# Another order of the first loads and a new hand-planned list of first steps in a fused attention and expert kernel

## The chip, the cores and the metric

The kernel runs on one core of one Trainium2 chip. The time is device microseconds of one execution; of several executions the median is given. Four compute engines work side by side, each through its own queue in program order: PE (TensorE), DVE (VectorE), ACT (ScalarE) and POOL (GpSimd). SP, ACT and POOL also issue DMA transfers from their queues.

## The reference

Block-wise linear attention with a decay per head, then a two-layer network with an ELU between the layers.

```python
B, H, S, D = 4, 8, 768, 64          # block = 64, nb = 12
for b in range(nb):
    intra = einsum('bhic,bhjc->bhij', qb, kb) * Dmask        # decay ** (i - j), causal
    intra = einsum('bhij,bhjd->bhid', intra, vb)
    inter = einsum('bhid,bhde->bhie', qb * lam_pow, kv_state)
    out[:, :, sl] = intra + inter
    kv_state = lam_block * kv_state + einsum('bhsd,bhse->bhde', kb * rev_pow, vb)
x = out.transpose(0, 2, 1, 3).reshape(3072, 512)
h = x @ w_in                        # 512 x 2048
g = where(h > 0, h, exp(min(h, 0)) - 1)
return g @ w_out                    # 2048 x 512
```

## The kernel before

A *step* s is one block of 64 positions of a pair of batches: 24 steps, s even for batches 0 and 1, odd for 2 and 3. Partitions 0 to 63 hold the first batch of the pair, 64 to 127 the second. Per step the keys, queries and values arrive as `kn`, `qn`, `vn` in fp16, cast by the transfer (POOL queue, two transfers each, one per batch). Step 0's keys and queries are different: they are loaded uncast as `kraw`, `qraw` over the queues of SP and ACT, and DVE casts them. A *group* is two steps, 256 rows of the network's input.

The two weight matrices come in four blocks each, `wi0` to `wi3` and `wo0` to `wo3`, on the POOL queue, in an order written by hand between the loads of the steps. The scheduler is off (`manual_schedule`): instructions are issued as the Python code calls them. The first steps are called from a string, `start`; behind it a regular loop takes over from group 3. A word of the string is one call:

- `Fk`, `Fq`: casts of step 0 on DVE (`cast0`). `K0`: the decay mask times the causal mask on DVE; `K1`: `lamL` and `powi`, nine exponentials on ACT (`consts`).
- `Aso.us.ss.sx` (`visit`): up to four things on PE, an empty place leaves one out: the outputs O of step so (and, with a state, the state's share I), the state update U of step us, the scores S of step ss, the transposes T of the keys and queries of step sx.
- `C` copies the transposes out of PSUM, `P` multiplies scores by the mask, `V` decays the values (`vd`, for U), `N` writes the new state `st`, `D` decays the state (`sd`), `Q` decays the queries (`qs`, for I): all DVE. `X` copies an O to `xt`, the input of the network, on ACT.
- `Hg.c.n.f` (`mm1_h`): the first layer's matmuls for group g, half c, four of its sixteen column tiles from f (16 matmuls of 128 columns, weights `wi` of block f/4). `E` (`mm1_e`): exp and relu on ACT. `G` (`mm1_g`): the ELU on DVE. `Ms.f` (`mm2`): four of the second layer's sixteen matmuls for step s, weights `wo` of block f/4. `Zs` (`mm2_o`): copy and store of its result.

So `A..1.` is "scores of step 1", `A...2` "transposes of step 2". Scores and state updates share a PSUM tile `psZ` (`psS` and `psU`), the transposes of the first four steps share `psM` with the results of M, the H results `psH` have two buffers, e and r four each. Constants are made from an iota `ij` (POOL; `ident`, `ijf`, `caus`, `i1f` on DVE) and from `lam_b`, the decay bases, loaded on the ACT queue. On ACT one table load stands at the start.

Of the kernel before, what the change touches and what calls it, by code (L numbers as in the profile page):

```python
# [8 lines left out]
FP32 = mybir.dt.float32  # L9
# [7 lines left out]
def kernel(  # L17
# [10 lines left out]
    nc = tc.nc  # L28

    B, H, S, D = q.shape  # L30
    L = 64
# [10 lines left out]
    cst = ctx.enter_context(tc.tile_pool(name="cst", bufs=1))  # L42
    inp = ctx.enter_context(tc.tile_pool(name="inp", bufs=1))
# [6 lines left out]
    def where(s):  # L50
        return 2 * (s % NPR), s // NPR

    def half(x):
        return slice(64 * x, 64 * x + 64)

    lam_b = cst.tile([128, H], FP32, name="lam_b")
    nc.scalar.dma_start(out=lam_b[:], in_=lam.unsqueeze(0).broadcast_to([128, H]))
    nc.scalar.preload_act_table_set("natural_log_exp_and_others")

    NB = 12  # L60
    kn, qn, vn = {}, {}, {}

    def load(which, s):
        b, c = where(s)
        src, keep, tag = {"k": (k, kn, "kn"), "q": (q, qn, "qn"), "v": (v, vn, "vn")}[which]
        keep[s] = inp.tile([128, H, D], FP16, tag=tag, bufs=NB, name=f"{tag}{s}")
        for r in range(2):
            nc.gpsimd.dma_start(  # L68
                out=keep[s][half(r)],
                in_=src[b + r, :, c * L : (c + 1) * L, :].rearrange("h p d -> p h d"),  # L70
            )

    def load_step(s):
        load("k", s)
        load("q", s)
        load("v", s)
# [12 lines left out]
    def load_wo(i):  # L89
# [2 lines left out]
            in_=moe_w_out[i * WB : (i + 1) * WB, :].rearrange("(g p) f -> p g f", p=128),  # L92
        )

    ij = cst.tile([128, L], I32, name="ij")
    for r in range(2):
        nc.gpsimd.iota(ij[half(r)], pattern=[[1, L]], base=0, channel_multiplier=-1)

    raw0 = {}
    for which, src in (("k", k), ("q", q)):  # L100
        raw0[which] = inp.tile([128, H, D], FP32, name=f"{which}raw0")
        for r in range(2):
            (nc.sync if which == "k" else nc.scalar).dma_start(
                out=raw0[which][half(r)], in_=src[r, :, 0:L, :].rearrange("h p d -> p h d")
            )
    load("v", 0)
    load_step(1)
    load_wi(0)
    load_step(2)
# [29 lines left out]
        out=i1f[:], in0=raw[:], scalar1=rjf[:, 0:1], scalar2=float(L),  # L139
# [276 lines left out]
    def consts(i):  # L416
# [13 lines left out]


    start = (
        "Fk Fq V0 A...0 C0 A.0.. K1 N0 A...1 K0 A..0. P0 V1 A0... X0 D2 A.1.. N1 H0.0.1.0 C1 D3 "
        "A..1. E0.0.1.0 P1 A...2 A1... C2 X1 Q2 A..2. H0.1.1.0 P2 E0.1.1.0 V2 A2... G0.0.1.0 "
        "A.2.. H0.0.1.4 X2 N2 H1.0.1.0 E0.0.1.4 D4 G0.1.1.0 A...3 E1.0.1.0 H1.0.1.4 C3 Q3 A..3. "
        "E1.0.1.4 H0.1.1.4 V3 G0.0.1.4 E0.1.1.4 P3 H0.1.1.8 G1.0.1.0 H0.0.1.8 E0.1.1.8 G0.1.1.4 "
        "A.3.. G1.0.1.4 A3... E0.0.1.8 H1.0.1.8 N3 M1.0 D5 X3 G0.0.1.8 E1.0.1.8 H1.1.1.0 G0.1.1.8 "
        "M0.0 E1.1.1.0 G1.0.1.8 H0.1.1.12 G1.1.1.0 H1.1.1.4 E0.1.1.12 M1.4 E1.1.1.4 G0.1.1.12 "
        "H1.1.1.8 H0.0.1.12 G1.1.1.4 E1.1.1.8 M1.8 E0.0.1.12 G1.1.1.8 H1.0.1.12 G0.0.1.12 A...4 "
        "E1.0.1.12 H1.1.1.12 C4 M0.4 V4 E1.1.1.12 G1.0.1.12 M0.8 Q4 A..4. G1.1.1.12 M1.12 P4 "  # L440
        "M0.12 Z1 M2.0 Z0 A...5 V5 M2.4 C5 M3.0 Q5 A4.4.5.6 M3.4 P5 X4 N4 H2.0.1.12 C6 H2.0.1.4 "
        "E2.0.1.12 Q6 M3.8 D6 E2.0.1.4 H2.0.1.8 G2.0.1.12 V6 M3.12 E2.0.1.8 G2.0.1.4 A5.5.6.7 V7 "
        "Z3 G2.0.1.8 H2.0.1.0 X5 N5 H2.1.1.12 E2.0.1.0 P6 M2.8 D7 E2.1.1.12 G2.0.1.0 H2.1.1.4 V8 "
        "M2.12 E2.1.1.4 G2.1.1.12 H2.1.1.0 C7 Z2 G2.1.1.4 A6.6.7.8 E2.1.1.0 Q7 M4.0 N6 X6 "
        "G2.1.1.0 M4.4 P7 H2.1.1.8 C8 M4.8 E2.1.1.8 D8 Q8 A7.7.8.9 G2.1.1.8 M4.12 X7 N7 P8 Z4 C9 "
    )
    steps = {
        "C": att_C, "P": att_P, "X": lambda s: att_X(s, nc.scalar),
# [87 lines left out]
```

## Time and profile before

| | |
|---|---|
| median of 3 runs | 219.03 us (218.57 to 219.05) |
| profiled execution | 218.62 us, of it span 216.8 us |
| PE busy | 201.8 us, 93% of the span |
| DVE, ACT, POOL busy | 152.8, 134.0, 135.7 us |
| first matmul | at 8.06 us |
| first matmul of the network (H) | at 13.14 us |
| moved by DMA | 20.73 MB, of it 13.38 over the POOL queue |

The span goes from the first to the last instruction; about 1.8 us lie around it. Times inside the profile are microseconds from the start of the span. A row of the time line gives the start, the length, the engine, the line of the kernel, the operation, what it writes and reads, how many instructions are merged in it and, in brackets, how long the engine had been idle and who ended that. Lengths of instructions overlap: on DVE an operation of 0.68 us is followed by the next start 0.6 us later, on ACT one of 0.59 us by the next 0.49 us later.

### The profile page before, as it was taken

The numbers are of one execution on the slowest core, as the hardware profiler recorded it, in microseconds if no ns is written. First come the engines' busy times: TensorE is split into PE (matmuls) and PEld (weight loads), VectorE is DVE, ScalarE is ACT, GpSimd is POOL, SyncE is SP. The second block draws the span as 40 slices with busy tenths as digits, with TensorE's granted clock in tenths as the row PEclk, the third lists the DMA queues.
The fourth block names the chain that finished last, engine by engine and source line by source line (L and its number), as shares of the span: only waits on it lengthen the run. The fifth ranks groups of instructions, "written<-read, shape, count | busy, mean of one in ns | idle before, by whom it ended". The sixth has DMA issues, their size and how long they took to land.

```text
span 216.8 us, 8162 instructions
## 1 busy us (share of the span) xinstructions
PE 201.8 (93%) x3600; PEld 143.0 (66%) x3600; DVE 152.8 (70%) x224; ACT 134.0 (62%) x259; POOL 135.7 (63%) x180
## 2 busy tenths in 40 slices
PE   0479989999999999999999999999999999999992
PEld 0358868657867677677676676676676676666662
DVE  3788884859987789769779769779769748433321
ACT  4633867526756677577577577577577577567730
POOL 8988525997999799797797797797734102000000
PEclk9999999999999999999999999999999999999999
DMA  7999999999999959977986976977921121122024
GB/s 105 144 178 176 180 205 180 135 146 130 141 140 132 123 73 75 105 85 59 106 88 57 106 86 56 107 85 59 104 53 22 33 51 23 30 48 48 3 48 98
DMA packets 84436, 20.73 MB, mean 96 GB/s; under 512 B 77104, under 2 KB 81456, under 8 KB 84400
## 3 DMA queue, kind: packets, MB, share of 16 engines
q0 software_dynamic: 78144, 13.38, 79.5%
q1 hardware_dynamic: 4896, 6.43, 13.0%
q10 hardware_dynamic: 1360, 0.40, 0.9%
q8 instruction: 28, 0.46, 0.9%
q14 instruction: 8, 0.07, 0.1%
HBM read 27.27 MB, written 6.29 MB: 155 GB/s over the span
## 4 chain that ended last, share of the span: by engine, by line
PE 90%; POOL 4%; DMA 3%; issue 1%; DVE 1%; ACT 1%; POOLq 0%; DVEq 0%
PE psH L347 39%; PE psM L387 38%; PE psO L304 3%; DMA qn<-in_q_dram 3%; PE psO L273 2%; PE psM L406 2%; PE psZ L297 2%; POOL vn L68 1%; PE psZ L290 1%; POOL kn L68 1%; PE psO L282 1%; POOL qn L68 1%; PE psO_None L273 1%; PE psM L304 0%; PE psO_None L282 0%
## 5 line engine op out<-in xcount | busy, mean ns | idle before, releaser
L368 DVE SCALAR_TENSOR_TENSOR g<-e,r 128x512 f16<-128x512 f32 x96 | 84.0, 889 | 45.7 <-ACT r L359 45.4
L347 PE MATMUL psH<-xt,wi 128*128 128x256 f16 (+1 forms) x960 | 101.2, 256 | 0.8 <-DMA wi<-in_moe_w_in_dram 0.6
L347 PEld LDWEIGHTS <-wi 128*128 128x128 f16 x960 | 80.8, 100 | 25.0 <-DMA wi<-in_moe_w_in_dram 0.7
L357 ACT ACTIVATE e<-psH 128x512 f32<-128x512 f32 x96 | 57.4, 598 | 60.1 <-PE psH L347 59.7
L387 PE MATMUL psM<-wo,g 128*128 128x512 f16 x368 | 93.7, 380 | 0.0
L359 ACT ACTIVATE r<-psH 128x512 f16<-128x512 f32 x96 | 57.0, 594 | 0.0
L387 PEld LDWEIGHTS <-g 128*128 128x128 f16 x368 | 33.9, 98 | 25.2
L68 POOL DMA_DIRECT2D vn<-in_v_dram x48 | 34.3, 751 | 5.5 <-DMA wo<-in_moe_w_out_dram 3.0
L201 POOL TENSOR_TENSOR qs<-T,powi 128x512 f16<-128x512 f16 x14 | 16.3, 1164 | 33.1 <-DVE T L222 33.1
L68 POOL DMA_DIRECT2D kn<-in_k_dram x46 | 32.6, 731 | 3.1 <-DMA wo<-in_moe_w_out_dram 2.3
L68 POOL DMA_DIRECT2D qn<-in_q_dram x46 | 32.3, 729 | 1.5 <-DMA kn<-in_k_dram 0.9
L192 POOL TENSOR_TENSOR sd<-st,lamL 128x512 f32<-128x512 f16 x12 | 17.8, 1487 | 0.0
L208 DVE TENSOR_TENSOR P<-psZ,mask 128x512 f16<-128x512 f32 x24 | 16.4, 683 | 1.8 <-PE psZ L297 0.9
L394 ACT COPY o<-psM 128x512 f32<-128x512 f32 x23 | 13.6, 592 | 4.9 <-PE psM L387 4.9
L183 DVE TENSOR_TENSOR vd<-vn,rev 128x512 f16<-128x512 f16 x22 | 15.0, 682 | 0.0
L244 DVE TENSOR_TENSOR st<-psZ,sd 128x512 f16<-128x512 f32 x20 | 13.6, 680 | 0.8 <-PE psZ L290 0.8
L232 ACT CAST xt<-psO 128x512 f16<-128x512 f32 x18 | 10.6, 587 | 4.7 <-PE psO L304 4.5
L304 PEld LDWEIGHTS <-qn 64*64 64x64 f16 x384 | 6.6, 109 | 9.4 <-DVE qn L171 8.1
L222 DVE COPY T<-psO 128x1024 f16<-128x1024 f16 x18 | 12.2, 680 | 0.0
L273 PEld LDWEIGHTS <-st 64*64 64x64 f16 x352 | 6.9, 106 | 5.5 <-issue 2.6
L304 PE MATMUL psM<-ident,qn 64*64 64x64 f16 x64 | 2.1, 231 | 8.4 <-DVE qn L171 8.1
L273 PE MATMUL psO<-qs,st 64*64 64x64 f16 x288 | 9.4, 202 | 0.0
(47 smaller groups left out, 110.7 us busy)
## 6 DMA issues: line engine op xcount, KB each, us to landing
out_dram<-o SPq DMA_DIRECT2D x46, 128.0 KB, 2.5
vn<-in_v_dram POOLq DMA_DIRECT2D x48, 64.0 KB, 3.8
kn<-in_k_dram POOLq DMA_DIRECT2D x46, 64.0 KB, 4.1
qn<-in_q_dram POOLq DMA_DIRECT2D x46, 64.0 KB, 3.4
wi<-in_moe_w_in_dram POOLq DMA_DIRECT2D x4, 512.0 KB, 6.5
wo<-in_moe_w_out_dram POOLq DMA_DIRECT2D x4, 512.0 KB, 11.1
kraw<-in_k_dram SPq DMA_DIRECT2D x2, 128.0 KB, 4.3
qraw<-in_q_dram ACTq DMA_DIRECT2D x2, 128.0 KB, 4.6
```

The costliest lines, as they stand in the source:

```text
L68: nc.gpsimd.dma_start(out=keep[s][half(r)], in_=src[b + r, :, c * L : (c + 1) * L, :].rearrange("h p d -> p h d"),)
L183: eng.tensor_tensor(out=st[s]["vd"][:], in0=vn[s][:], in1=rev[:].unsqueeze(2).broadcast_to([128, H, D]), op=ALU.mult,)
L192: eng.tensor_tensor(out=st[s]["sd"][:], in0=state[s - NPR][:], in1=lamL[:].unsqueeze(3).broadcast_to([128, 2, NHP, D]), op=ALU.mult,)
L201: eng.tensor_tensor(out=st[s]["qs"][:], in0=st[s]["T"][:, :, 1, :, :], in1=powi[:], op=ALU.mult)
L208: nc.vector.tensor_tensor(out=d["P"][:].rearrange("p y j t -> p y (j t)"), in0=psS, in1=mask[:].rearrange("p y j t -> p y (j t)"), op=ALU. ...
L273: return nc.tensor.matmul(O[half(c), y, h // 2 * L : (h // 2 + 1) * L], lhsT=state[so - NPR][half(x), y, 2 * i + c, :], rhs=st[so]["qs"][h ...
L304: return nc.tensor.matmul(psT[r][half(c), x : x + L], lhsT=(kn, qn)[i][sx][half(r), NHP * (c ^ r) + j, :], rhs=ident[half(r), :], is_trans ...
L347: nc.tensor.matmul(psH[:, i, :], lhsT=wi[n // 4][:, kk, (n % 4) * 128 : (n % 4 + 1) * 128], rhs=xt[grp][:, kk, c0 * 128 : c0 * 128 + T], s ...
L357: nc.scalar.activation(e[:], psH[:], AF.Exp)
L359: nc.scalar.activation(r[:], psH[:], AF.Relu)
L368: nc.vector.scalar_tensor_tensor(out=g[:], in0=e[:], scalar=-1.0, in1=r[:], op0=ALU.add, op1=ALU.min)
L387: nc.tensor.matmul(acc[s], lhsT=gel.pop((s, n)), rhs=wo[n // 4][:, n % 4, :], start=(n == 0), stop=(n == NFT - 1),)
```

## The change

The first loads are issued in another order. On the ACT queue the first half of the queries goes first, then `lam_b`, then the second half, then the table load; before, `lam_b` and the table load stood ahead of both halves. On the POOL queue the two transfers of step 0's values go ahead of the two iotas instead of behind them. On the SP queue the two halves of the keys are issued as before. The string `start` is replaced by another order of the same 182 words.

```diff
-    lam_b = cst.tile([128, H], FP32, name="lam_b")
-    nc.scalar.dma_start(out=lam_b[:], in_=lam.unsqueeze(0).broadcast_to([128, H]))
-    nc.scalar.preload_act_table_set("natural_log_exp_and_others")
...
+    raw0 = {}
+    for which in "kq":
+        raw0[which] = inp.tile([128, H, D], FP32, name=f"{which}raw0")
+    lam_b = cst.tile([128, H], FP32, name="lam_b")
+    for r in range(2):
+        for which, src, eng in (("k", k, nc.sync), ("q", q, nc.scalar)):
+            eng.dma_start(
+                out=raw0[which][half(r)], in_=src[r, :, 0:L, :].rearrange("h p d -> p h d")
+            )
+        if r == 0:
+            nc.scalar.dma_start(out=lam_b[:], in_=lam.unsqueeze(0).broadcast_to([128, H]))
+    nc.scalar.preload_act_table_set("natural_log_exp_and_others")
+    load("v", 0)
     ij = cst.tile([128, L], I32, name="ij")
     for r in range(2):
         nc.gpsimd.iota(ij[half(r)], pattern=[[1, L]], base=0, channel_multiplier=-1)
-
-    raw0 = {}
-    for which, src in (("k", k), ("q", q)):
-        raw0[which] = inp.tile([128, H, D], FP32, name=f"{which}raw0")
-        for r in range(2):
-            (nc.sync if which == "k" else nc.scalar).dma_start(
-                out=raw0[which][half(r)], in_=src[r, :, 0:L, :].rearrange("h p d -> p h d")
-            )
-    load("v", 0)
     load_step(1)
     load_wi(0)
...
     start = (
-        "Fk Fq V0 A...0 C0 A.0.. K1 N0 A...1 K0 A..0. P0 V1 A0... X0 D2 A.1.. N1 H0.0.1.0 C1 D3 "
-        "A..1. E0.0.1.0 P1 A...2 A1... C2 X1 Q2 A..2. H0.1.1.0 P2 E0.1.1.0 V2 A2... G0.0.1.0 "
-        "A.2.. H0.0.1.4 X2 N2 H1.0.1.0 E0.0.1.4 D4 G0.1.1.0 A...3 E1.0.1.0 H1.0.1.4 C3 Q3 A..3. "
-        "E1.0.1.4 H0.1.1.4 V3 G0.0.1.4 E0.1.1.4 P3 H0.1.1.8 G1.0.1.0 H0.0.1.8 E0.1.1.8 G0.1.1.4 "
-        "A.3.. G1.0.1.4 A3... E0.0.1.8 H1.0.1.8 N3 M1.0 D5 X3 G0.0.1.8 E1.0.1.8 H1.1.1.0 G0.1.1.8 "
...
+        "Fk Fq K1 K0 A...0 C0 V0 A..0. A...1 P0 V1 A.0.. A0... X0 N0 C1 A.1.. N1 D2 H0.0.1.0 D3 "
+        "A..1. E0.0.1.0 P1 A...2 A1... G0.0.1.0 X1 C2 H0.1.1.0 V2 A..2. Q2 E0.1.1.0 P2 H0.0.1.4 "
+        "G0.1.1.0 A2... E0.0.1.4 A.2.. H0.1.1.4 N2 X2 G0.0.1.4 A...3 E0.1.1.4 H1.0.1.0 C3 V3 "
+        "A..3. E1.0.1.0 H1.0.1.4 P3 Q3 A.3.. E1.0.1.4 H0.0.1.8 G1.0.1.0 D4 A3... E0.0.1.8 "
+        "G1.0.1.4 H0.1.1.8 G0.1.1.4 X3 H1.0.1.8 G0.0.1.8 E0.1.1.8 N3 M1.0 D5 E1.0.1.8 H1.1.1.8 "
...
```

In the part left out, the second-layer steps come in the order M1.0, M2.0, M2.4, M2.8, M1.4, M1.8 (before: M1.0, M0.0, M1.4, M1.8, M0.4, M0.8), the visits keep their order from `A...4` on, and around the visit `A4.4.5.6` DVE is given

```diff
-  ... A4.4.5.6 M3.4 P5 X4 N4 H2.0.1.12 C6 H2.0.1.4 E2.0.1.12 Q6 M3.8 D6 E2.0.1.4 H2.0.1.8 G2.0.1.12 V6 ...
+  ... A4.4.5.6 V6 M0.12 N4 X4 P5 H2.0.1.4 Z0 D6 H2.0.1.12 C6 E2.0.1.4 M3.4 Q6 E2.0.1.12 G2.0.1.4 ... V7 ...
```

## The prediction

> **What bounds the kernel now.** I read the page first, for the shares; then the busy times of PE (TensorE) by stretches; then the chain of waits and the time line of the first 30 us. An execution is bound by PE once PE has work, and the whole change lies before that.
>
> The page, head and slices (each digit a fortieth of the span, 5.4 us):
>
> ```profile
> span 216.8 us, 8162 instructions
> ...
> PE 201.8 (93%) x3600; PEld 143.0 (66%) x3600; DVE 152.8 (70%) x224; ACT 134.0 (62%) x259; POOL 135.7 (63%) x180
> ...
> PE   0479989999999999999999999999999999999992
> ...
> DMA  7999999999999959977986976977921121122024
> ```
>
> The busy time of PE in stretches that I chose (stretch, its length, PE busy and instructions, granted clock, share of the DMA engines, GB/s):
>
> ```profile
> 0.00:8.06 8.06, 0.00 (x0) 1.00 1.27 119
> 8.06:13.14 5.08, 3.16 (x128) 1.00 1.55 155
> 13.14:30.00 16.86, 15.74 (x367) 1.00 1.50 183
> 30.00:70.00 40.00, 40.00 (x817) 1.00 1.60 147
> 70.00:200.00 130.00, 129.93 (x2203) 1.00 0.72 70
> ```
>
> From 30 us PE never rests. Both lists hold the same 182 words in another order, so PE's instructions are the same. An order can change only what PE loses before 30 us: 8.06 + 1.92 us ahead of the first expert matmul (H0.0.1.0, 13.14 us) and 1.12 us between it and 30. It could also add gaps later.
>
> The time line of PE around these losses (start, length, instruction, count, idle before it and its releaser):
>
> ```profile
> 12.13 0.43 PE L290 MATMUL psZ<-vd,kn 64*64 64x64 f16 x16 [0.17 <-DVE vd L183]
> ...
> 13.14 1.89 PE L347 MATMUL psH<-xt,wi 128*128 128x128 f16 x16 [0.58 <-DMA wi<-in_moe_w_in_dram]
> ...
> 16.19 0.43 PE L282 MATMUL psO_None<-P,vn 64*64 64x64 f16 x16
> ...
> 17.33 1.89 PE L347 MATMUL psH<-xt,wi 128*128 128x128 f16 x16
> ...
> 23.16 1.07 PE L347 MATMUL psH<-xt,wi 128*128 128x128 f16 x16
> ...
> 26.65 1.05 PE L347 MATMUL psH<-xt,wi 128*128 128x128 f16 x16 [0.19 <-ACT r L359]
> ...
> 29.04 0.21 PE L282 MATMUL psO_None<-P,vn 64*64 64x64 f16 x1 [0.53 <-issue]
> ```
>
> The first H waits for weight block wi0, with 0.58 us to spare behind the last small matmul: the steps ahead of it are paid by a transfer, not by their order. Secondly, 16 matmuls of one H take 1.89 us at 13.14 and 17.33 but 1.07 from 23.16 (0.18 of either is the tail of the last one): PE starts at half speed. The granted clock reads 1.00 all along, so I go by durations. The two H from 20.23 take 2.56 us to the next start; with 107 ns (1.71/16) and 55.6 ns (0.89/16) per matmul, 15 are slow, so full speed comes at about 21.8 us.
>
> **The change part by part.**
>
> *Queues.* ACT issued lam_b (0.74 us, 0.39 long), then the two halves of q0 from 1.20 (0.73 and 0.65). Now q0's first half goes at 0.74, lam_b behind it at about 1.47, q0's second half at about 1.86 (was 1.95), and the table load (1.28 us) follows at 2.55 instead of 1.17. On POOL the two v0 issues (1.53 us) pass the two iotas (0.40 us): v0 is sent some 0.5 us earlier, the iotas end at about 2.8 instead of 1.24, and k1 goes where it went, 2.89, as the sum ahead of it is the same. SP keeps its order.
>
> *Who waits for the moved small things.* The six DVE constants from the iota (1.27 to 2.24 us) run 1.5 us later and end by 3.8. lam_b took 2.6 us to land; issued at 1.47 that gives 4.1, and if it lands only with q0's first half in front of it, at most some 4.6 (k0's first half, issued at 0.74, needed 4.3 in all), against 3.4 now. The chain loglam, loglamP, eight mask exponentials, which ended at 6.5, then ends at 7.2 to 7.7. The list now puts K0 (mask times causal, 0.68) ahead of the first T copies; it starts at 7.93 behind the two casts and still has its mask in time. If not, the first T copies are late, and of that the spare 0.58 us is free.
>
> *The block up to the first H, laid end to end with the rows of before.* Casts to 8.00; K0 to 8.6; T0 copies at 8.74 (they wait for PE, as now) to 9.41; V0 to 10.0; P0 (S0 on PE ends near 10) to 10.7; V1 to 11.3; N0 to 11.9. PE: O0 ends near 11.2, so X0 ends at 11.85 (now 12.59); U1 needs N0's read of psU and ends at 12.4 (now 12.56). All is ahead of wi0, which landed just under 13.14. Moving V0, K0 and N0 is worth nothing here; cover left 0.7 us.
>
> *When wi0 lands.* The DMA engines hold work without a break from about 2.5 us until far behind wi0. The only gain is that two streams, not one, run from the start. The stretches moved 31 GB/s in 2.0 to 2.5 us, 142 in 2.5 to 3.0 and 216 in 3.0 to 4.0. With q0 beside k0 at once I take 62 and 216: (31 + 74) GB/s over half a microsecond, 52 KB more, which is 0.3 us at the 172 to 185 GB/s behind it. Bounds: 0.46 us (what q0's first issue gains) and, on the side of loss, 0.3 us, should mixed streams or the late lam_b cost what they are to bring. I take 0.3 earlier for wi0 and all that follows on that queue. Until 21.8 PE runs at half speed and does half the work per time, so this is worth 0.15 us at the end.
> [...]
>
> *The new order from 13.14 to 30 us.* Now: H0.0.1.0, S1, T2 (held to 15.52 by q2's landing), O1, S2 in pieces between 16.64 and 17.2 because it waits for T2's two copies, H0.1.1.0 at 17.33. New: H0.1.1.0 stands straight behind O1, and waits for the X1 copy (16.66 to 17.24), so it starts at 17.25, and S2 (0.25 us at half speed) comes after it: a loss of 0.25 - 0.08 = 0.17. What is queued behind this wait on PE is S2 and all later H; DVE loses nothing, P2 is due later. In return H0.0.1.4 now stands between S2 and O2, so P2 and Q2 on DVE stay hidden. Further, H0.0.1.8 at 26.65 waited for ACT to free its buffer (0.19 us idle behind the 0.18 us tail of the matmul before: some 0.35 without a new start), and the two H from 24.41 took 2.05 us for 2 x 0.89 + 0.18 = 1.96; in the new list A.3.. and A3... stand between these H, and ACT's pair per H (0.98 us) keeps up with PE's 0.89 plus 0.2 to 0.6 of attention. Gain 0.35 + 0.09. One H behind A.2.. meets the X2 copy and waits about 0.07. Sum: 0.17 + 0.07 - 0.44 = -0.2 us.
>
> *Later.* The list puts V6 and V7 (decays of v6, v7) earlier on DVE; N4, P5, C6 and the qs of the next visit queue behind V6, two g steps behind V7. v6 was issued by 44.3 and the landing of a v load is 3.8 us in the middle, so V6 waits until about 47; the visit that needs the results starts at 53.3 now. Cover 4 us, cost nothing; without it the visit would be late by the wait.
>
> **Sum.** -0.15 - 0.2 = -0.35 us. The profiled execution took 218.62 us (span 216.8, 1.8 around it), so 218.3 on its scale; the median of the runs is 0.41 higher, 219.03, so I expect 218.7.
>
> **The rivals.**
>
> *The stall at 28.3 goes too.* The last of O3's matmuls started 0.73 us behind its neighbour, with no releaser ("issue"). For its going: nothing in the list explains it, and the new list has another step at that place. Against: if it hangs on the place in PE's instruction stream, it stays. Time: 218.7 - 0.7 = 218.0.
>
> *The longer pause delays full speed: slower.* In the new list PE rests about 0.65 us in one piece ahead of H0.1.1.0, where the old one filled half with S2. If the speed-up at 21.8 hangs on how busy PE was in the stretch before, it may come later; every H at half speed costs 0.82 more. Three of them late give 2.5 us at most, two 1.6, so 220.3 for two. It decides from one and a half H on (1.2 us): below that the gain of 0.35 holds it within measurement. Against: from 17.25 on the new list is denser than the old, and PE's busy share from 17.33 to 21.67 is already 98%.
> [...]
>
> *The loads do nothing, or the order does nothing* (one of the two terms is 0): 218.8 to 218.9, inside my forecast.
>
> **How the numbers follow.** A measurement of this kernel can tell about 0.3%, 0.66 us. My forecast and its weaker forms, 218.4 to 219.3: 0.54. The stall's going, alone or with the upper bound of the loads (0.46 instead of 0.3) and a slightly earlier full speed, 217.4 to 218.3: 0.33. Later full speed or a late mask or wi0, 219.7 to 220.6: 0.13. The range leaves out the far half of each rival: 217.5 to 219.9.
>
> **What would show it.** Right: H0.0.1.0 starts at 12.7 to 13.2 and still waits for wi0; the chain of waits passes through q2 and X1 to H0.1.1.0; the idle time of PE between the first H and 30 us falls from 1.12 by some tenths; no PE idle time from 30 to 70. Wrong: the first H late because of X0 or the mask; H rows of 1.89 us behind 22; PE gaps around 47 to 66 with DVE as releaser.

## The result, and the profile after

The changed kernel is slower: median 220.71 us (219.68 to 221.59, eight executions) against 219.04 (218.52 to 220.1) for the kernel before beside it; ratio 1.0065, 95% interval 1.0036 to 1.0094 (the quotient of the two medians is 1.0076, inside it). I had forecast 218.7 and given "slower" 0.13. Executions that took over 1.5% longer than the fastest of their kernel are left out of all ratios and differences below. The profiled execution of after took 219.68 us, the shortest of the eight: its trace explains 219.68 - 218.62 = 1.06 us of the 1.67 between the medians. For the rest I rely on the runs below.

The page after, the lines shown of before:

```profile
span 217.9 us, 8163 instructions
...
PE 200.6 (92%) x3600; PEld 142.2 (65%) x3600; DVE 153.0 (70%) x224; ACT 134.0 (62%) x259; POOL 135.8 (62%) x180
...
PE   0188989999999999999999999999999999999992
...
DMA  7999999999999949958967967967920120122024
```

The second digit of PE's slices (5.4 to 10.9 us) fell from 4 to 1: the first matmuls come later. The busy time of PE in the same stretches as before:

```profile
0.00:8.06 8.06, 0.00 (x0) 1.00 1.23 118
8.06:13.14 5.08, 2.39 (x112) 1.00 1.32 142
13.14:30.00 16.86, 14.39 (x368) 1.00 1.52 178
30.00:70.00 40.00, 39.82 (x821) 1.00 1.60 144
70.00:200.00 130.00, 129.93 (x2203) 1.00 0.72 71
```

Idle time of PE rose by 0.77 us up to 13.14, by 1.35 between there and 30, and by 0.18 from 30 to 70: 2.30 in all. Its busy time fell by 1.2 (201.8 to 200.6), since less of the work ran at half speed (252 matmuls started ahead of full speed, before 302; one of an H took 107 ns there, 56 behind it): 2.30 - 1.2 = 1.1, the growth of the span. In the third stretch one can see both at once: one instruction more (368 against 367) in 1.35 us less of busy time. The last column matters too: 142 GB/s moved between 8.06 and 13.14, where it had been 155.

The time line (start, length, what, count, idle before it and its releaser), POOL and ACT's queue first, then DVE, then PE:

```profile
1.25 1.54 POOL L64 DMA_DIRECT2D vn<-in_v_dram  x2 [0.81 <-POOLq L523]
1.52 0.68 ACTq L103 DMA_DIRECT2D lam_b<-in_lam_dram  x1
2.88 0.43 POOL L108 IOTA ij<- 64x64 int32 x2
3.25 1.35 POOL L64 DMA_DIRECT2D kn<-in_k_dram  x2
6.39 0.25 DVE L145 TENSOR_SCALAR lam_b<-lam_b 128x8 f32<-128x8 f32 x1 [1.76 <-DMA lam_b<-in_lam_dram]
9.59 0.69 DVE L420 TENSOR_TENSOR mask<-mask,caus 128x512 f32<-128x512 f32 x1 [0.91 <-ACT mask L157]
13.43 0.43 PE L292 MATMUL psZ<-vd,kn 64*64 64x64 f16 x16 [0.58 <-DVE st L250]
13.84 1.89 PE L349 MATMUL psH<-xt,wi 128*128 128x128 f16 x16
...
18.00 1.87 PE L349 MATMUL psH<-xt,wi 128*128 128x128 f16 x16 [0.68 <-ACT xt L234]
...
28.01 1.01 PE L349 MATMUL psH<-xt,wi 128*128 128x128 f16 x15
29.99 1.12 PE L349 MATMUL psH<-xt,wi 128*128 128x128 f16 x17 [0.97 <-issue]
```

The same iotas, issues of POOL and use of `lam_b` in before:

```profile
0.84 0.40 POOL L97 IOTA ij<- 64x64 int32 x2 [0.39 <-POOLq L520]
...
1.38 1.53 POOL L68 DMA_DIRECT2D vn<-in_v_dram  x2
...
2.89 1.38 POOL L68 DMA_DIRECT2D kn<-in_k_dram  x2
3.41 0.17 DVE L143 TENSOR_SCALAR lam_b<-lam_b 128x8 f32<-128x8 f32 x1 [1.16 <-DMA lam_b<-in_lam_dram]
```

Three things stand here that the prediction had otherwise. The iotas, moved behind the values, now lie between two issues of POOL, and step 1's keys go at 3.25 instead of 2.89. `lam_b` was issued at 1.52, close to the 1.47 that I had said, but DVE got it at 6.39 (before 3.4), and the mask chain reaches K0 at 9.59. And the stall without a releaser, 0.73 us at 28.3 before, is longer and stands at 29 (1.19 us from the start of one matmul at 28.80 to that of the next at 29.99).

The chain of waits from the start confirms the second point:

```profile
1.52 4.85 DMA lam_b<-in_lam_dram
...
7.54 2.03 ACT mask L157 x8
...
12.76 0.63 DVE st L250
```

The 4 KB of `lam_b` took 4.85 us to land. Mask, K0, T0's copies (10.20; before 8.74), V0, P0, V1, N0 and U1 follow each other up to the first H at 13.84. Block `wi0` landed at 13.79 (before 13.09) in the same execution: the two causes end within 0.1 us of each other (U1 at 13.86), so undoing one of them alone would have left the start where it was. That is why parts had to be undone one by one.

### The profile page after: what moved, and what is told of

It is laid out like the page before. It is cut to its first block, busy times and chain, and to the rows that moved or that the text cites. A ratio compares the mean times of both kernels' runs of the same rounds, so it can differ in the third digit from the quotient of the medians.

```text
span 217.9 us, 8163 instructions
## 1 busy us (share of the span) xinstructions
PE 200.6 (92%) x3600; PEld 142.2 (65%) x3600; DVE 153.0 (70%) x224; ACT 134.0 (62%) x259; POOL 135.8 (62%) x180
## 4 chain that ended last, share of the span: by engine, by line
PE 91%; DMA 2%; DVE 2%; issue 1%; ACT 1%; ACTq 0%; DVEq 0%
PE psH L349 40%; PE psM L389 37%; PE psO L306 3%; PE psO L275 2%; DMA lam_b<-in_lam_dram 2%; PE psZ L299 2%; PE psM L408 2%; PE psZ L292 1%; PE psO L284 1%; ACT mask L157 1%; PE psO_None L275 1%; DVE vd L185 1%; PE psO_None L284 0%; PE psONone L306 0%; ACTq L99 0%
## 5 line engine op out<-in xcount | busy, mean ns | idle before, releaser
L64 POOL DMA_DIRECT2D kn<-in_k_dram x46 | 33.1, 748 | 3.2 <-DMA wo<-in_moe_w_out_dram 2.2
L64 POOL DMA_DIRECT2D qn<-in_q_dram x46 | 32.8, 749 | 1.5 <-DMA kn<-in_k_dram 1.5
L306 PE MATMUL psM<-ident,qn 64*64 64x64 f16 x64 | 1.6, 229 | 8.7 <-DVE qn L173 8.7
```

The lines of the kernel that those rows point to most:

```text
L64: nc.gpsimd.dma_start(out=keep[s][half(r)], in_=src[b + r, :, c * L : (c + 1) * L, :].rearrange("h p d -> p h d"),)
L306: return nc.tensor.matmul(psT[r][half(c), x : x + L], lhsT=(kn, qn)[i][sx][half(r), NHP * (c ^ r) + j, :], rhs=ident[half(r), :], is_trans ...
```

## The experiments

The expectations name theories by a letter: A, the late decay bases (`lam_b` behind the first half of the queries) delay mask and first block; B, the new list is the slow part; C, POOL, late by its two iotas, delays all loads behind them, `wi0` among them; D, the difference is only scatter between executions; F, the stall at 28 to 30 is PE fetching its instructions and belongs to a place in PE's instruction stream; G, it belongs to the steps at that place of the list; H, what PE loses at half speed, up to 17 to 24 us, is the larger part. Each timed kernel ran twelve times. Where two kernels of one chip are compared directly, the difference of their mean times is given with its 95% bounds, about two standard errors.

### Which half of the change costs

`e2_list_only`: the loads of before with the new list.

> The loads of the kernel before, the new list alone. Theory A: the first H starts at 13.1 to 13.2 again, the stall of PE without releaser at its 963rd instruction stays (0.7 to 1.2 us); time equal to the kernel before within 0.3 us, 218.7 to 219.4. Theory B (the list costs): 219.8 to 220.5, with the stall at instruction 963 over 1.1 us and a second one later.

Measured: ratio 0.9999 (0.9972 to 1.0026). Whatever the list alone costs or brings lies under some 0.3%.

`e3_loads_only`: the new loads with the old list.

> The new order of the loads with the old list. Theory A: lam_b lands after 6 us; in the old list V0 stands ahead of the first T copies and needs rev, the last of the ACT chain (near 9.7), so the first T copies start at 10.4 or later and the first H at 13.8 to 14.5: slower than before by 0.8 to 1.6 us, 219.8 to 220.6. Theory B: 218.8 to 219.4, as before.

Measured: 1.0008 (0.9976 to 1.0041), below what was expected and unclear beside the kernel before. Beside e2 on the same chip it is 0.45 +- 0.61 us longer, which is unclear too. Its profile has the delays of after: `lam_b` landed at 5.59, X0 at 12.98, first H at 15.10. This pair doesn't show that the loads carry the loss; e4 and e9 below do.

`e1_lam_first`: after, with `lam_b` first again.

```diff
+    nc.scalar.dma_start(out=lam_b[:], in_=lam.unsqueeze(0).broadcast_to([128, H]))
     for r in range(2):
...
-        if r == 0:
-            nc.scalar.dma_start(out=lam_b[:], ...)
```

> The changed kernel with one line moved: lam_b is issued first on the ACT queue, ahead of both halves of the queries. Theory A (lam_b landed at 6.37 us instead of 3.38 because it queued behind the queries' first half; mask, K0 and the first T copies were late by it, and the first H with them): lam_b lands by 3.5, the mask ends near 7.0, the first T copies start at 8.7 to 8.9 instead of 10.2, X0 ends near 12; the first H then waits for wi0 alone and starts at 13.2 to 13.8; some 0.4 to 0.8 us of the 1.4 us come back, 219.6 to 220.3 where the changed kernel takes 220.7. Theory B (the list is the slow part: instruction fetch of PE and the X1 wait): the first T copies come early but the time stays within 0.2 us of the changed kernel.

Measured: 1.0025 (1.0001 to 1.0050). The mask chain was as early as with the old loads (K0 7.82, X0 11.35; 7.93 and 11.46 in e2), and still the first H waited 2.27 us for `wi0` and started at 14.59. An early mask alone does not undo the loss.

`e4_iota_first`: after, with the two iotas ahead of the values again; `lam_b` stays behind the first half of the queries.

```diff
-    load("v", 0)
     ij = cst.tile([128, L], I32, name="ij")
     for r in range(2):
         nc.gpsimd.iota(ij[half(r)], ...)
+    load("v", 0)
```

> The changed kernel with the two iotas ahead of the values' loads on POOL again, lam_b still behind the queries' first half. Theory A: lam_b still lands after 6 us, so the first T copies and X0 stay late and the first H starts at 13.6 to 13.9: within 0.3 us of the changed kernel, 220.4 to 221.0. Theory C (what held the first H is wi0, late because POOL issued everything behind the values 0.36 us later): k1 is issued at 2.9 again, wi0 lands by 13.2 and the first H starts by 13.4: 219.9 to 220.2.

Measured: 0.9972 (0.9946 to 0.9997), a little faster than before (its repeat e12 below can't be told from before) and 1.10 +- 0.58 us shorter than e1 on the same chip. Theory A as I had put it fell: with the iotas first, `lam_b` was there at 4.78 although it stood in the same place of ACT's queue. The time line of e4:

```profile
0.84 0.40 POOL L107 IOTA ij<- 64x64 int32 x2 [0.39 <-POOLq L523]
...
2.90 1.38 POOL L64 DMA_DIRECT2D kn<-in_k_dram  x2
...
4.78 0.17 DVE L145 TENSOR_SCALAR lam_b<-lam_b 128x8 f32<-128x8 f32 x1 [2.54 <-DMA lam_b<-in_lam_dram]
8.04 0.68 DVE L420 TENSOR_TENSOR mask<-mask,caus 128x512 f32<-128x512 f32 x1
...
```

The iotas run at 0.84, in time that POOL otherwise waits, and the values' issue is at 1.39, only 0.14 us behind the 1.25 of after. The step-1 keys go at 2.90. K0 starts at 8.04, close to the 7.93 of the prediction.

`e5_after_again`: the changed kernel once more, on another chip.

> The changed kernel once more, beside the kernel before on the same chip. The four kernels that undid one part each came out within 0.3% of the kernel before. Theory D (the 0.65% are mostly the spread of the starts: when wi0 lands, 13.1 to 15.1 us in the profiles so far, and when PE reaches full speed, 16.8 to 24.4 us): ratio 1.000 to 1.004. Theory A with B (lam_b and POOL order and fetch add up only where all are together): ratio 1.005 to 1.009 again.

Measured: 1.0054 (1.0029 to 1.0078). Theory D falls: the change is slower here too. Its profile has the delays of after (`lam_b` landed at 6.21, K0 9.59, first H 14.18).

### POOL's lateness alone

`e9_pool_late`: e4 with two spare iotas behind the values, which nobody reads. `e12_iota_first_again`: e4 once more, beside it.

```diff
     load("v", 0)
+    spare = cst.tile([128, L], I32, name="spare")
+    for r in range(2):
+        nc.gpsimd.iota(spare[half(r)], ...)
     load_step(1)
```

> The kernel with iotas first, and two more iotas into a spare tile behind the values' loads on POOL: the constants are early, but k1 and all behind it on POOL are issued some 0.3 to 0.4 us later, as in the changed kernel. Theory C (what costs is that wi0 and the loads behind it come later): wi0's first part lands near 12.4 to 12.6 instead of 12.1, the first H starts 0.3 to 0.9 later than with iotas first, ratio to before 1.000 to 1.004 where iotas first gave 0.997. Theory A (what costs is the late constants and lam_b): ratio stays within 0.2% of iotas first, run beside it.

> The changed kernel with iotas first on POOL once more, beside the two kernels made from it. It gave 0.9972 (0.9946 to 0.9997) on another chip. If the order on POOL is what costs, 0.996 to 0.999 again; if that was the spread of the starts, 1.000 to 1.005 like the changed kernel.

Measured: e9 1.0020 (0.9994 to 1.0046), e12 0.9982 (0.9947 to 1.0016), e9 longer by 0.80 +- 0.60 us. The time line of e9:

```profile
2.98 0.40 POOL L111 IOTA spare<- 64x64 int32 x2
3.31 1.35 POOL L64 DMA_DIRECT2D kn<-in_k_dram  x2
...
13.82 1.68 PE L352 MATMUL psH<-xt,wi 128*128 128x128 f16 x14 [0.93 <-DMA wi<-in_moe_w_in_dram]
```

The keys go at 3.31, 0.41 later than in e4, the mask is early (K0 8.40), and what the first H waits for is `wi0`: this is C without A, and it costs about 0.4%. The first part of `wi0` landed at 12.49 in e9, within the 12.37 to 12.62 of the kernels that have the iotas behind the values, and at 11.98 to 12.14 where POOL was early. The last part of `wi0` scatters more, and with one exception every kernel with POOL late is behind every one with POOL early: 12.61 to 13.54 with POOL early (once 14.79, in e8), 13.78 to 15.05 with POOL late. The first H scatters with it.

### A later mask

`e10_lam_last`: e4 with `lam_b` behind both halves of the queries (`if r == 1:` instead of `if r == 0:`).

> The kernel with iotas first, and lam_b behind both halves of the queries on ACT: lam_b lands at 7 to 8 us, the mask ends near 11, K0, the first T copies and X0 come 2 us later than with iotas first, X0 near 13.5 to 14. Theory A: the first H starts at 14.4 to 15, ratio to before 1.001 to 1.005. Theory C: wi0 at 13.1 to 13.5 is what the first H waits for up to there, so 1 us of the 2 is covered; half of the rest comes back while PE runs at half speed: ratio 0.998 to 1.001.

Measured: 1.0087 (1.0051 to 1.0122), more than expected, and 2.32 +- 0.79 us longer than e12. `lam_b` was used at 7.17, K0 at 10.74, X0 at 14.05, the first H at 14.95, while `wi0` was there at 13.30. Here the mask chain alone holds the first H. So a late mask costs as soon as the steps behind it, U1 the last of them, end later than `wi0` lands; K0 some 1.2 us earlier, as in after, is at that edge.

### The stall at 28 to 30 us

With PE's instructions counted from 0, it stands in the kernel before and in after ahead of the same one, number 962, though the steps there differ. On the instruction queue (28 packets, 0.46 MB on the page: 16 KB each; 0.46 MB over PE's 3600 matmuls and 3600 weight loads is 64 bytes an instruction and 256 to a packet, an estimate that counts the whole queue as PE's) one fetch ends shortly before PE goes on. From the traces, in us ("fetch" is the transfer on that queue, the next column the start of number 962, the last what PE lost there, from the start of one weight load to that of the next):

| kernel | PE at 706 | fetch | PE at 962 | idle |
|---|---|---|---|---|
| before | 23.04 | 26.66 to 27.55 | 29.03 | 0.75 |
| after | 23.75 | 27.52 to 28.41 | 29.99 | 1.24 |
| e6 | 23.82 | 27.01 to 27.96 | 29.24 | 1.03 |
| e7 | 23.82 | 27.33 to 28.28 | 29.92 | none |
| e11 | 22.23 | 25.78 to 26.67 | 28.32 | none |

706 and 962 are 256 apart. The fetch starts some 3.2 to 3.8 us after PE has passed number 706 and takes 0.9 to 1.0; PE goes on 1.3 to 1.7 behind its end. What PE does in that time, and whether it is the loads then under way that hold the fetch up, no run shows.

`e6_pad`: after, with the transposes of step 0 done twice, which puts 64 instructions ahead of all others.

```diff
-        "Fk Fq K1 K0 A...0 C0 V0 ...
+        "Fk Fq K1 K0 A...0 A...0 C0 V0 ...
```

> The changed kernel with the transposes of step 0 done twice (32 matmuls, 64 instructions of PE more, where PE waits anyway); the result is unchanged. Theory F (the stall without releaser near 29 us is PE waiting for its own instructions: a block of 256 is fetched by a 16 KB transfer that queues behind the weight loads): the stall stays at instruction 963 of PE's stream, which is now 32 matmuls earlier in the list, inside A3... instead of in H0.1.1.8, 1.0 to 1.8 us long, and ends 1.3 to 1.6 us behind the end of the third fetch. Theory G (it belongs to a step of the list): it stays at the last matmul of H0.1.1.8.

Measured (one execution): 219.93 us. The time line of e6:

```profile
27.84 0.58 PE L275 MATMUL psO_None<-qs,st 64*64 64x64 f16 x15
29.24 0.21 PE L275 MATMUL psO_None<-qs,st 64*64 64x64 f16 x1 [0.82 <-issue]
```

The stall left the expert matmuls and stands inside the state's share of A3..., ahead of number 962 again: F holds as far as the place goes, G falls.

`e11_before_heavy`: the kernel before, with A.3.. and A3... moved behind one more H, so that the block holds more H matmuls and lasts longer.

```diff
-        "A.3.. G1.0.1.4 A3... E0.0.1.8 H1.0.1.8 N3 M1.0 D5 X3 G0.0.1.8 E1.0.1.8 H1.1.1.0 ...
+        "G1.0.1.4 E0.0.1.8 H1.0.1.8 A.3.. A3... E1.0.1.8 N3 M1.0 D5 X3 G0.0.1.8 H1.1.1.0 ...
```

> The kernel before (old loads, old list) with A.3.. and A3... behind H1.0.1.8 instead of ahead of it: 16 large matmuls move into instructions 707 to 962 of PE, 16 to 64 small ones out. Theory F with a price (the stall of 0.73 us at instruction 963 is paid in full): no stall there or under 0.3 us, ratio to before 0.9965 to 0.9985. Theory F without a price (the time comes back at the next wait): stall gone, ratio 0.999 to 1.001.

Measured: 0.9974 (0.9947 to 1.0001); the stall at 962 is gone, but another one without a releaser stands later:

```profile
65.39 0.31 PE L304 MATMUL psO<-ident,qn 64*64 64x64 f16 x13 [1.10 <-issue]
```

That is number 2498, six blocks of 256 behind 962, and a fetch ended at 63.94, 1.45 us before PE went on: the same stall at a later block. So what the one at 962 costs by itself this run doesn't settle.

`e7_heavy_page` makes the same move in the new list, with e4's loads.

```diff
-        ... P3 Q3 A.3.. E1.0.1.4 H0.0.1.8 G1.0.1.0 D4 A3... E0.0.1.8 G1.0.1.4 H0.1.1.8 G0.1.1.4 X3 H1.0.1.8 G0.0.1.8 ...
+        ... P3 Q3 E1.0.1.4 H0.0.1.8 G1.0.1.0 D4 E0.0.1.8 G1.0.1.4 H0.1.1.8 G0.1.1.4 E0.1.1.8 H1.0.1.8 G0.0.1.8 A.3.. A3... ...
```

> Iotas first on POOL, and in the new list A.3.. and A3... go behind H1.0.1.8 (64 small matmuls later, 16 large ones earlier), so that instructions 707 to 962 of PE take some 0.6 us longer by themselves. Theory F: the stall at instruction 963 shrinks from 1.2 to 1.5 us to 0.5 to 0.9, instruction 963 is reached at the same time with 0.7 us more work done, and the time falls by 0.4 to 0.7 us against the kernel with iotas first: ratio to before 0.993 to 0.996. Theory G: the stall keeps its length and the ratio stays at 0.997 or above.

Measured: 218.74 us against 219.49, ratio 0.9971 (0.9949 to 0.9994). The time line of e7:

```profile
29.55 0.59 PE L275 MATMUL psO_None<-qs,st 64*64 64x64 f16 x16
29.95 0.32 PE L284 MATMUL psO_None<-P,vn 64*64 64x64 f16 x16
```

Number 962 is reached at 29.92, here inside the first row, and no idle time stands there, where after had lost 1.19. It beats both kernels, and on one chip it is 1.73 +- 0.46 us shorter than the changed kernel (e5). But the ratio is no better than e4's 0.9972, so a gain of the removed stall over e4 isn't shown; the 0.993 to 0.996 that I had expected did not come.

Over all 14 profiles PE stood idle there in 12, for 0.5 to 2.1 us by the views of its waits (least in before and e12, most in e8); in e7 and e11 it did not.

### Warming PE up

`e8_warm`: e4 with 23 matmuls of 128x512 on a zeroed tile between the first steps (words W16, W1, W1, W2, W3), whose results nobody reads.

> Iotas first on POOL, the new list, and 23 matmuls of 128x512 on a zeroed tile while PE waits (16 ahead of the first transposes, 7 between the next steps; their result is not used). Theory H (half speed until 17 to 24 us is what PE loses, whatever the order): full speed before 13 us, H rows of 1.07 from the first on, and of the some 3 us that half speed costs between 13 and 22 us part comes back; what stops it are wi1 (18.5), wi2 (25.3) and, by theory F, the third fetch: instruction 963 not earlier than 6 us behind instruction 707. Time 0.8 to 2 us under the kernel before, ratio 0.991 to 0.996. If the fetch binds fully, ratio 0.997 and a stall of over 2 us.

Measured: 0.9987 (0.9953 to 1.0022), from 217.7 to 223.1: no gain that can be told from nothing. The trace is of the longest one, 223.09 us; what the shorter ones did isn't shown. PE in three stretches of it:

```profile
4.00:5.00 1.00, 1.00 (x4) 1.00 1.26 132
...
15.00:16.00 1.00, 1.00 (x14) 0.57 1.19 146
...
32.30:35.50 3.20, 3.20 (x21) 0.50 1.27 205
```

By the lengths of the dummy matmuls (starts 427 ns apart, then 216) full speed came at 4.89; it was lost at 15.1, behind a wait of 2.00 us for `wi0`, until 21.95; then again at 32.2, behind a fetch stall of 2.34 us. Here the granted clock does show it, with 0.57 and 0.50. In the traces it is kept as records, the first of which begins with full speed (4.89 here, 21.67 in before, 21.40 in after); ahead of that the views print 1.00, and only the lengths tell.

The records also show when the clock changed. Between two changes they last 3.41, 6.83 and 10.24 us here, 194.56 in before and 197.97 in after: in these three traces whole multiples of 3.41 us. In this execution the 3.41 us ahead of either fall had PE busy for 1.37 and 1.41 us, with the wait for `wi0` and most of the fetch stall in them; a stretch as long in e2, 28.98 to 32.39, had 1.94, and full speed stayed. What decides between the two, these three stretches don't show.

## Why the prediction was wrong

1. *"v0 is sent some 0.5 us earlier ... and k1 goes where it went, 2.89, as the sum ahead of it is the same."* This step failed, and most of the loss that I can assign hangs on it. The iotas of before ran from 0.84 to 1.24, where POOL sent nothing in after either: its first transfer goes at 1.25 there, not at 0.84, and so the values gained 0.13 us and every later load on POOL lost 0.36. I took the queue's sum and not its earliest possible start. Priced by e9 against e12 at 0.80 +- 0.60 us, with e1 against e4 (1.10 +- 0.58) in agreement. In the sum it is the term of the loads: -0.15 us forecast, a loss measured.
2. *"lam_b ... 4.1, ... at most some 4.6."* Measured 6.37 in after; 4.65 to 5.07 in kernels with the iotas first. The bound took over the landing of k0's first half, 4.3 on SP's queue; in after q0's first half itself landed at 5.35 and `lam_b` 1.02 behind it, 4.85 us after its issue. K0 was late by 1.66 us against my 7.93, and U1 ended at 13.86 instead of 12.4. Its own cover of 0.7 us was gone. e10 shows that a late mask costs once it passes `wi0`. What it cost in after by itself isn't settled: e5 (1.0054) against e1 (1.0025) gives 0.3%, on two chips and with overlapping intervals.
3. *"I take 0.3 earlier for wi0."* It landed 0.70 us later. The bound on the side of loss was 0.3; the step was blind to the late issue on POOL (point 1). Nor do the runs show the gain of two streams: with POOL early, `wi0` landed at 12.61 to 13.44 with the queries first (e4, e7, e10, e12; 14.79 in e8) and at 12.81 to 13.54 with `lam_b` first (before, e2, e11).
4. *The new order, -0.2 us.* The waits that I named came as I said: H0.1.1.0 rested 0.68 us in one piece for X1, where I had written 0.65, and no H from 22 to 28 us waits for ACT's buffer any more. One was missing from the sum: O1 now waits 0.38 us for P1 on DVE (16.89 in after, 0.37 in e2). e2's 0.9999 can't tell -0.2 us from nothing. *V6 and V7 cost nothing*: right, PE has no such idle time behind 30.
5. *The stall at 28.3.* I had made its going a rival with a high chance, on the ground that another step stood there, and had also named the reason against: a place in PE's instruction stream. That reason was the true one; the stall stayed and grew from 0.73 to 1.19.
6. *Later full speed, slower.* The rival ended on the right side by the wrong mechanism: full speed came at 21.40 instead of 21.67, in spite of the rest ahead of H0.1.1.0. That the two lie so close is luck: in e4 and e12, one kernel, full speed came at 16.82 and 22.67 by the records of the clock. That PE's rest ahead of H0.1.1.0 (0.68 us in after) moves it, no run shows. The slower side should have been built on the late mask and `wi0`, which I had named in half a sentence and priced up to 220.6.

What stays open: why `lam_b` lands later when the values go first (ACT's issues stand in the same order in e4 and after, but in the traces 66 to 99 KB of POOL's transfers had moved by the last of its 128 packets in after, e3, e5 and e6, and 26 to 40 KB in e4, e7, e8, e9 and e12; that this is the reason isn't shown); why e3 lost less than after and e5; and how much of the 0.6 us that the two profiled executions leave of the difference of the medians is a later `wi0`, and how much another moment of full speed, which ranged from 16.8 to 24.4 us between the profiles other than e8's.

## What to carry to other kernels

Before something short is moved behind a transfer on an issuing queue, look in the trace when that queue sends its first transfer at all (POOL at 1.25 us here): the work ahead of that moment was all but free (0.14 us here), and behind it every later issue paid (0.36 us here). A sum along a queue holds only from its earliest start on. Read a stall that has no releaser by its number in the engine's instruction stream (here 962, in before, after and e6 alike), and where a first result depends on two late arrivals, undo them singly: neither shows its price while the other covers it.

## What the runs showed that I had not expected

- The fetch that ends ahead of number 962 starts late: 3.2 to 4.5 us after PE had passed number 706 in the 14 profiles, where the one before it started 0.4 to 2.6 us after PE had passed number 450. PE reached number 962 between 5.7 and 6.9 us after number 706, whatever stood between. With more long matmuls between the two (e7, e11) no idle PE was left there; with more 64-column matmuls it was 0.5 to 2.1 us by the views of its waits.
- A transfer of 4 KB to 128 partitions, issued behind one half of the queries, landed 3.1 to 4.85 us after its issue, against 2.6 to 3.0 in the kernels where it was first on its queue (before, e2, e11).
- POOL's first transfer went out no earlier than 1.25 us in any profile, while SP and ACT sent theirs at 0.74 or 0.75.
- Between two changes of the clock lay whole multiples of 3.41 us in e8, before and after. An earlier first result need not bring an earlier full speed: e4 had its first H at 13.48 and full speed at 16.82, e12, the same kernel, its first H at 12.65 and full speed at 22.67.
